# Decayed linear attention and a sine MLP on one core: new orders for all queues, other engines and load sizes in the opening, and the last tile's first store on SyncE

## The chip, the cores and the metric

One NeuronCore of a Trainium2 (trn2) chip. The metric is the device time of one execution in microseconds; the kernel before was run three times and its median is quoted. A profile is of one execution, which has its own time.

## The reference, cut to what matters

```python
# q, k, v: [4 batches, 8 heads, 768 positions, 64]; lam: [8]; block = 64
for b in range(12):                       # 12 blocks of 64 positions
    intra = einsum('bhic,bhjc->bhij', qb, kb) * Dmask     # lam**(i-j) where i >= j, else 0
    intra = einsum('bhij,bhjd->bhid', intra, vb)
    inter = einsum('bhid,bhde->bhie', qb * lam_pow, kv_state)      # lam**(pos+1)
    out[b] = intra + inter
    kv_state = lam**64 * kv_state + einsum('bhsd,bhse->bhde', kb * rev_pow, vb)
x = out.transpose(0, 2, 1, 3).reshape(3072, 512)
h = x @ w_in                              # 512 x 2048
g = h + sin(alpha * h)**2 / (alpha + 1e-9)
result = g @ w_out                        # 2048 x 512, float32 [3072, 512]
```

The inputs are float32; the kernel multiplies in bfloat16 and adds up in float32.

## The kernel before, in words

**The MLP.** The 3072 tokens go in six chunks c of 512. Step `Ac.m` (L1219) makes block m of 128 of the 2048 hidden features for chunk c: four matmuls over the 512 inputs, each 512 columns wide. Where its name ends in h0 or h1 it makes one half of the tokens for two blocks, with 256 columns. ACT takes the sine (`sin`, L1231), POOL, DVE or ACT squares it (`sq`, L1238 on ACT, L1239 on the others; the tables SQ0 and SQ1 say who), and DVE makes g out of the square and the PSUM (`g`, L1243), which frees the PSUM bank. Step `Bc.s.m` (L1296) adds four feature blocks into the output tile s of 128 tokens; after the fourth, ACT copies the tile out (L1312) and issues its store of 256 KB (L1315). The last tile of the last chunk, B5.3, is done in `last_tile` by column pieces instead: piece 0 has 256 columns, 1 and 2 have 128 each (CUTS). Each piece has 16 matmuls (L1264), a copy (L1272, on ACT for 0 and 2, on DVE for 1; tags o23.0 to o23.2) and a store of its own (L1275; tags st23.0 to st23.2; on ACT's queue for 0 and 2, on SP's for 1).

**The attention.** It makes x, transposed, chunk by chunk, in 24 quads t of 128 tokens by four head pairs. The first eight quads are `quad0`: quads 0 to 3 make chunk 0, 4 to 7 chunk 1. For quad t: the loads of q, k and v (`load_quad`, L780 for q, L786 for k and v; float32, tags such as "quad q3.0", "quad k2.1"); the scaling by powers of lam (`qs` L825, `ks` L838, the latter in two halves .0 and .1 where the engine table names two engines); the cast of v (`vs`, L852 on ACT, L855 elsewhere); transposes on PE of k and q (`Tk`, `Tq`, L866) and their copies out of PSUM (`cTt.1` for k, `cTt.0` for q, L869); the scores (`S`, L909) and their mask on DVE (`mask`, L914); the state's matmuls (`Z`, L926) with two copies (`Zi`, L945); the inter part (`I`, L956), the intra part (`O`, L971), the copy to x (`x`, L988); the running state on DVE (`Zt.1`, L999) and its bf16 copies (`Zs`, L1011). Quads 0 and 1 start from an empty state; 2 and 3 continue from theirs. S0 needs cT0.0, cT0.1 and the q parts; Z needs `ks` and `vs`; O needs the mask and `vs`. After x0 to x3 the A steps of chunk 0 can run: A0.4 and others begin on the half that x0 and x1 give, A0.2 needs all four. Later quads (8 to 23) are transposed by DMA (tags DT).

**Weights.** POOL issues software DMAs for w_in (tags w0, w0b, w1 to w3) and w_out (w4 to w7), which cast to bf16 on the way.

**What sets the order.** Every operation is recorded with what it reads and writes (`rec`). The class `Program` then walks through them with modelled times; each engine's sequence, including its DMA issues, is written out by hand in the table ORDER, one list for PE, DVE, ACT, POOL and SP (c0, c1, ... are the constants). The dependencies become semaphore waits. Four things follow from that table and the model's times: which PSUM bank each step gets (six banks for all but the scores of the opening); how many filler matmuls on zeros (L641) go in front of a PE step that would wait; the loads that GATE names wait for the named step before SP issues them, as does everything behind them on SP's queue; and a POOL step that the model starts less than 0.3 us after a DVE step marked `port="whole"` gets a wait for that DVE step. SP also holds back while more than 2300 descriptors of its are under way.

In PE's list of before the opening runs: Tk2, Tq1, Tq2, Tq3, Tq0, Tk0, S0, Tk1, Z1, Z0, S1, alpha T, I0, O0, I1, S2, Z3, Tk3, O1, Z2, S3, A0.4h0e (the first half of A0.4's h0), I2, A0.4h0, I3, O2, O3, A0.2h0, ... The first loads on SP are q2.0, k0.0, k2.1 (one pair of head pairs, 128 KB), q3.0, q1.0, q0.0, k2.0, v0.0, v2.0, k3.1 (the other 128 KB), v2.1, v0.1, q4.0, k6.1, v4.0, k4.0; k0.1 is issued by ACT.

Of the kernel before, what the change touches and what calls it, by code (L numbers as in the profile page):

```python
# [37 lines left out]
    ENG0=({'c': 'DVE', 'k': 'POOL', 'p': 1, 'q': ('POOL', 'DVE'), 'v': 'POOL', 'w': 'AD', 'z': 'DA'},
          {'c': ('ACT', 'DVE'), 'k': 'DVE', 'p': 2, 'q': 'DVE', 'v': 'ACT', 'w': 'DA', 'z': 'DD'},
          {'c': ('DVE', 'ACT'), 'k': ('DVE', 'POOL'), 'p': 2, 'q': 'DVE', 'v': 'ACT', 'w': 'DD', 'z': 'AD'},  # L40
          {'c': ('DVE', 'ACT'),
           'k': ('POOL', 'DVE'),
           'p': 2,
           'q': ('DVE', 'POOL'),
           'v': 'ACT',
           'w': 'DA',
           'z': 'AA'}),
    X0=('ACT', 'DVE', 'DVE', 'ACT'),
    ENG1=({'c': 'ACT', 'k': ('POOL', 'DVE'), 'p': 0, 'q': 'DVE', 's': 0, 'v': 'POOL', 'w': 'AA', 'z': 'DD'},
          {'c': ('DVE', 'ACT'),  # L50
# [6 lines left out]
           'z': 'AD'},  # L57
          {'c': ('DVE', 'ACT'),
           'k': ('POOL', 'DVE'),
           'p': 2,  # L60
           'q': ('POOL', 'DVE'),
           's': 0,
           'v': 'ACT',
           'w': 'DD',
           'z': 'AA'},
          {'c': ('ACT', 'DVE'),
           'k': ('DVE', 'POOL'),
           'p': 1,
           'q': ('DVE', 'POOL'),
           's': 0,  # L70
           'v': 'DVE',
           'w': 'AD',
           'z': 'DD'}),
# [1381 lines left out]
```

## Time and profile before

| | us |
|---|---|
| median of 3 runs | 213.82 (213.73 to 213.84) |
| the profiled execution | 213.67 |
| its span, first to last instruction | 211.8 |
| ACT busy (L1231, the sines, 65.7 of it) | 128.7 |
| DVE busy (L1243, the g steps, 70.2 of it) | 128.5 |
| POOL busy (L1239, the squares, 70.6 of it) | 120.7 |
| matmuls of the A steps, L1219 | 88.1 |
| matmuls of the B steps, L1296 | 83.6 |
| fillers on zeros, L641, 45 groups | 10.7 |

The granted TensorE clock of the profiled execution was 0.998. The page's second part cuts the span into 40 slices of 5.3 us and gives each engine's busy tenths in each:

```profile
PE   7798999999999999999999999999999999999994
PEld 5455756555774555444554455454544544444454
DVE  4598899678889971285753475474556521456700
ACT  3146899835599755767648756757786434646231
POOL 3772174511537772899945899687397335144500
```

The first four to five digits of each row are the opening; the last is the end. A row of the timeline has the start, the length, the engine, the line, the operation with output and inputs, the shapes, the count of merged instructions, and in brackets the idle time ahead of it and what ended that.

### The profile page before, as it was taken

How to read it: one execution, taken by the hardware profiler on the slowest of the kernel's cores; microseconds unless marked ns; L12 is line 12 of the kernel's file. 1: busy time of each engine (PE TensorE's matmuls, PEld its weight loads, DVE VectorE, ACT ScalarE, POOL GpSimd, SP SyncE). 2: the span in 40 equal slices, each digit the busy share in tenths (PEclk: the TensorE clock that was granted, in tenths of full speed). 3: DMA queues.
4: the chain of work that ended last, by engine and by line, in shares of the span. 5: the costliest groups of instructions: out<-in, count | busy, mean ns of one | idle time of the engine just before them, and what ended most of it. 6: DMA issues, size and time to landing. Idle time of an engine off the chain costs nothing.

```text
span 211.8 us, 5201 instructions
## 1 busy us (share of the span) xinstructions
PE 202.6 (96%) x2108; PEld 108.9 (51%) x2139; DVE 128.5 (61%) x229; ACT 128.7 (61%) x246; POOL 120.7 (57%) x135
## 2 busy tenths in 40 slices
PE   7798999999999999999999999999999999999994
PEld 5455756555774555444554455454544544444454
DVE  4598899678889971285753475474556521456700
ACT  3146899835599755767648756757786434646231
POOL 3772174511537772899945899687397335144500
PEclk9999999999999999999999999999999999999999
DMA  6999999998999968899779999957033011101214
GB/s 182 314 238 235 208 251 237 216 223 169 244 182 197 190 117 190 200 199 197 189 154 209 198 183 240 177 137 171 3 99 148 4 50 50 53 0 50 101 54 149
DMA packets 86491, 33.92 MB, mean 160 GB/s; under 512 B 68274, under 2 KB 83522, under 8 KB 86466
## 3 DMA queue, kind: packets, MB, share of 16 engines
q1 hardware_dynamic: 77552, 22.88, 55.3%
q0 software_dynamic: 4752, 4.19, 12.1%
q10 hardware_dynamic: 4162, 6.50, 8.7%
q8 instruction: 17, 0.28, 0.6%
q14 instruction: 8, 0.07, 0.1%
HBM read 27.27 MB, written 6.29 MB: 158 GB/s over the span
## 4 chain that ended last, share of the span: by engine, by line
PE 85%; DVE 6%; DMA 2%; issue 2%; ACTq 1%; SPq 1%; ACT 1%; POOL 0%; POOLq 0%
PE M_ps L1219 39%; PE M_ps L1296 36%; DMA q<-in_q_dram 2%; PE M_ps L1120 2%; PE M_ps L1100 1%; DVE gT L1243 1%; PE A_ps L1080 1%; PE M_ps L866 1%; PE M_ps L971 1%; DVE S_m L1092 1%; DVE S_m L914 1%; PE M_ps L956 1%; PE M_ps L1264 1%; DVE q2o L825 1%; PE A_ps L909 1%
## 5 line engine op out<-in xcount | busy, mean ns | idle before, releaser
L1239 POOL TENSOR_TENSOR u<-t 128x512 bf16<-128x512 bf16 x69 | 70.6, 1041 | 55.0 <-ACT t L1231 51.7
L1243 DVE SCALAR_TENSOR_TENSOR gT<-u,r_sb,M_ps 128x512 bf16<-128x512 bf16 (+1 forms) x108 | 70.2, 684 | 45.1 <-POOL u L1239 43.8
L1219 PE MATMUL M_ps<-xT,w 128*128 128x512 bf16 (+1 forms) x425 | 88.1, 355 | 0.6 <-DVE gT L1243 0.2
L1296 PE MATMUL M_ps<-w,gT 128*128 128x512 bf16 x347 | 83.6, 379 | 2.5 <-issue 1.9
L1231 ACT ACTIVATE t<-M_ps,alpha_sb 128x512 bf16<-128x512 f32 (+1 forms) x108 | 65.7, 640 | 27.7 <-PE M_ps L1219 26.0
L1219 PEld LDWEIGHTS M_ps<-xT,w 128*128 128x128 bf16 x432 | 41.4, 98 | 40.1 <-DVE gT L1243 0.5
L1296 PEld LDWEIGHTS M_ps<-w,gT 128*128 128x128 bf16 x368 | 34.3, 98 | 39.2 <-DVE gT L1243 0.4
L1044 POOL TENSOR_TENSOR qk<-k,Lk 128x512 bf16<-128x512 f32 x16 | 16.6, 1044 | 9.9 <-DMA k<-in_k_dram 9.9
L1092 DVE TENSOR_TENSOR S_m<-A_ps,maskl 128x768 bf16<-128x768 f32 x16 | 15.3, 955 | 8.5 <-PE A_ps L1080 8.4
L1312 ACT COPY osb<-M_ps 128x512 f32<-128x512 f32 x20 | 11.7, 585 | 13.4 <-PE M_ps L1296 13.4
L1044 POOL TENSOR_TENSOR qk<-q,Lq 128x512 bf16<-128x512 f32 x16 | 16.6, 1041 | 2.2 <-DMA q<-in_q_dram 2.2
L1172 ACT CAST xT<-M_ps 128x512 bf16<-128x512 f32 x16 | 9.4, 586 | 13.3 <-PE A_ps L1080 11.4
L641 PE MATMUL M_ps<-zeros 128*128 128x512 bf16 (+1 forms) x45 | 10.7, 390 | 1.4 <-DVE zeros L702 1.2
L1195 ACT CAST Zq<-Zf 64x256 bf16<-64x256 f32 x24 | 9.6, 400 | 1.4 <-DVE Zf L1185 0.7
L914 DVE TENSOR_TENSOR S_m<-A_ps,maskq 128x1024 bf16<-128x1024 f32 x8 | 9.7, 1212 | 1.0 <-PE A_ps L909 0.5
L1239 DVE TENSOR_TENSOR u<-t 128x512 bf16<-128x512 bf16 x13 | 7.3, 560 | 4.4 <-ACT t L1231 4.4
L1055 ACT CAST v<-v 128x512 bf16<-128x512 f32 x16 | 9.7, 618 | 0.3 <-DMA v<-in_v_dram 0.2
L838 POOL TENSOR_TENSOR qk<-k,Lk 128x256 bf16<-128x256 f32 (+1 forms) x7 | 4.9, 703 | 8.6 <-DMA k<-in_k_dram 8.0
L1238 ACT ACTIVATE u<-t 128x512 bf16<-128x512 bf16 x14 | 8.7, 636 | 0.3
L869 ACT COPY qkT<-M_ps 128x512 bf16<-128x512 bf16 x5 | 2.9, 587 | 7.3 <-PE M_ps L866 7.3
L641 PEld LDWEIGHTS M_ps<-zeros 128*128 128x128 bf16 x48 | 4.6, 122 | 4.4 <-issue 1.7
L1189 DVE TENSOR_TENSOR Zf<-M_ps,Zf 128x256 f32<-128x256 f32 x10 | 4.2, 418 | 4.2 <-ACT xT L1172 4.2
(87 smaller groups left out, 139.8 us busy)
## 6 DMA issues: line engine op xcount, KB each, us to landing
out_dram<-osb ACTq DMA_DIRECT2D x23, 256.0 KB, 2.8
q<-in_q_dram SPq DMA_DIRECT2D x20, 256.0 KB, 4.8
k<-in_k_dram SPq DMA_DIRECT2D x34, 128.0 KB, 4.2
v<-in_v_dram SPq DMA_DIRECT2D x32, 128.0 KB, 4.0
v<-in_v_dram SPq DMA_DIRECT2D x8, 256.0 KB, 8.2
w<-in_moe_w_out_dram POOLq DMA_DIRECT2D x4, 512.0 KB, 11.5
k<-in_k_dram SPq DMA_DIRECT2D x6, 256.0 KB, 10.5
...
```

The costliest lines, as they stand in the source:

```text
L641: last = e.matmul(m_ps[i][:, 0:c], zeros[:, 0:128], zeros[:, 0:c])
L914: rec("DVE", lambda e: e.tensor_tensor(S_m[jm][:, :, :].rearrange("p (h a b) c -> p h a (b c)", h=2, a=2), Av().rearrange("p h (a x) -> p ...
L1044: rec(en, lambda e, L=L, gs=slice(g0, g0 + m): e.tensor_tensor(o[:, :, gs], i[:, :, gs], L, ALU.mult), *(((0.65, 0.58) if en == "DVE" else ...
L1055: rec("ACT", lambda e: e.copy(o, i), 0.613, 0.51, reads=rd, writes=[f"v2.{c}"], tag=f"vs{t}")
L1092: rec("DVE", lambda e: e.tensor_tensor(S_m[jm][:, :, :].rearrange("p (a b) c -> p a (b c)", a=4)[:, :, 0:192], A_ps[:, :, :].rearrange("p ...
L1195: rec(en, lambda e, rows=rows, en=en: (e.copy if en == "ACT" else e.tensor_copy)(Zq[jj][rows, :, rows], Zf[jj][rows, :, :].rearrange("p i ...
L1219: last = e.matmul(m_ps[vb.i][:, N * i:N * i + N], w1[:, kc, 128 * mm:128 * (mm + 1)], xT[x][:, kc, ts], start=(kc == 0 and i == 0), stop=( ...
L1231: rec("ACT", lambda e, i=i, mm=mm: e.activation(t16[tt][:, N * i:N * i + N], m_ps[vb.i][:, N * i:N * i + N], ACTF.Sin, scale=alpha_sb[:, m ...
L1239: return e.tensor_tensor(u16[tt][:, :], t16[tt][:, :], t16[tt][:, :], ALU.mult)
L1243: rec("DVE", lambda e, i=i, mm=mm: e.scalar_tensor_tensor(out=gT[g][:, mm, ts], in0=u16[tt][:, N * i:N * i + N], scalar=r_sb[:, mm:mm + 1] ...
L1296: last = e.matmul(m_ps[vb.i], gT[g][:, m, 128 * s4:128 * (s4 + 1)], w2[:, m, :], start=(m == 0 or (split and m == 8)), stop=(m == NM - 1 o ...
L1312: rec("ACT", lambda e: e.copy(osb[o][:, :], m_ps[vb.i]), 0.585, 0.48, reads=[vb.key], writes=[f"o.{o}"], frees=[vb], tag=f"o{gsi}")
```

## The change

The tables in TUNE get other values, the constants' DVE steps get a mark, and one line of `last_tile` names another engine. No step of the computation is added or taken away.

- LOADS0: the two loads of 128 KB "quad k2.1" and "quad k3.1" become one of 256 KB with the tag "quad k2.1", in the third place of SP's list.
- ENG0, ENG1, X0: who does which step of the opening. x1 and x2 go from DVE to ACT; vs0 from POOL to ACT, qs1 from DVE to POOL; cT0.0, Zi0.0, Zi1.0, Zi1.1 and Zs0.1 from DVE to ACT; cT2.1, cT1.0, cT3.1, Zi0.1 and Zi2.0 from ACT to DVE; ks4.0 from POOL to DVE and ks4.1 from DVE to POOL; some more for quads 4 to 7.
- SQ1: sq1.7 (ACT) and sq1.14 (DVE) go to POOL.
- GATE: k4.0 waits for Tk1, q6.0 for Tk3, v4.1 for O0, v6.0 for Tk2 (before: v4.0 for O2, k6.0 for mask3, v6.1 for Tk3). The table's other keys name no step that is recorded before their load and do nothing.
- EARLY: the places in the table SEQ at which the four quads of the opening are recorded; the order on the engines is ORDER's.
- ORDER: new lists for all five queues.
- `port="whole"` on the DVE steps that make the constants (memsets, copies, one add).
- `last_tile`: the store of piece 0 is on SP's queue; in ORDER the pieces' matmuls come as 1, 0, 2 (before 0, 2, 1), and ACT's list ends with o23.0, o23.2, st23.2.

```diff
-    SQ1=('ACT', 'DVE', 'POOL', 'POOL', 'ACT', 'POOL', 'POOL', 'ACT', 'DVE', 'ACT', 'ACT', 'POOL', 'POOL', 'ACT',
-         'DVE', 'DVE'),
+    SQ1=('ACT', 'DVE', 'POOL', 'POOL', 'ACT', 'POOL', 'POOL', 'POOL', 'DVE', 'ACT', 'ACT', 'POOL', 'POOL', 'ACT',
+         'POOL', 'DVE'),
...
-    EARLY=(0, 3, 1, 2),
+    EARLY=(0, 2, 2, 2),
...
-    GATE={'k6.0': 'mask3', 'q4.1': 'mask0', 'q6.1': 'A0.2', 'v4.0': 'O2', 'v6.0': 'A0.2', 'v6.1': 'Tk3'},
+    GATE={'k4.0': 'Tk1', 'q4.1': 'Tk2', 'q6.0': 'Tk3', 'q6.1': 'A0.2', 'v4.0': 'A0.2', 'v4.1': 'O0', 'v6.0': 'Tk2'},
...
-            ('q', 0, 1, 1), ('k', 1, 2, 1), ('v', 1, 2, 2), ('k', 1, 3, 1), ('v', 1, 0, 2), ('k', 0, 2, 2),
-            ('v', 0, 2, 2)],
+            ('q', 0, 1, 1), ('v', 1, 2, 2), ('k', 1, 2, 2), ('v', 1, 0, 2), ('k', 0, 2, 2), ('v', 0, 2, 2)],
...
-    X0=('ACT', 'DVE', 'DVE', 'ACT'),
+    X0=('ACT', 'ACT', 'ACT', 'ACT'),
...
-    ORDER={'ACT': ['lam', 'c0', 'quad k0.1', 'c11', 'c13', 'c14', 'cT2.1', 'alpha in', 'c17', 'vs1', 'cT1.0', 'Zi0.1',
-                   'alpha', 'x0', 'vs3', 'c16', 'Zs0.0', 'cT3.1', 'vs2', 'Zi3.1', 'Zs1.1', 'Zi3.0', 'Zi2.0', 'c29',
-                   'sin0.4h0', 'x3', 'sin0.2h0', 'sin0.5h0', 'sin0.7', 'sin0.3h0', 'sin0.1', 'sin0.4h1', 'sq0.1',
+    ORDER={'ACT': ['lam', 'c0', 'quad k0.1', 'c11', 'c14', 'c16', 'c13', 'vs0', 'cT0.0', 'alpha in', 'vs1', 'Zi0.0',
+                   'vs3', 'Zi1.0', 'Zi1.1', 'x0', 'Zs0.0', 'x1', 'Zi3.1', 'Zi3.0', 'Zs1.1', 'vs2', 'alpha', 'Zs0.1',
+                   'c17', 'c29', 'sin0.4h0', 'sin0.5h0', 'x2', 'x3', 'sin0.2h0', 'sin0.3h0', 'sin0.7', 'sin0.1',
...
-           'DVE': ['c1', 'c9', 'c25', 'c7', 'c2', 'c20', 'c23', 'c10', 'c12', 'qs1', 'c22', 'qs3', 'ks2.0', 'qs2',
-                   'cT2.0', 'cT3.0', 'c15', 'cT0.0', 'cT0.1', 'ks1', 'c19', 'c26', 'mask0', 'cT1.1', 'Zi1.0', 'Zi0.0',
-                   'Zi1.1', 'mask1', 'ks3.1', 'c31', 'Z0.1', 'mask2', 'x1', 'Zs0.1', 'c27', 'c24', 'Zi2.1', 'Zs1.0',
-                   'mask3', 'Z1.1', 'x2', 'Z3.1', 'qs4', 'Z2.1', 'Zs2.0', 'sq0.4h0', 'g0.4h0', 'g0.5h0', 'sq0.2h0',
+           'DVE': ['c2', 'c26', 'c1', 'c7', 'c23', 'c19', 'c9', 'c10', 'c25', 'c20', 'c15', 'c12', 'c27', 'qs3',
+                   'qs2', 'ks2.0', 'ks3.1', 'cT2.0', 'cT3.0', 'cT2.1', 'c24', 'cT0.1', 'cT1.0', 'Zi0.1', 'ks1',
+                   'mask0', 'cT1.1', 'mask1', 'Z0.1', 'cT3.1', 'Zs1.0', 'mask2', 'Z1.1', 'Zi2.1', 'Zi2.0', 'mask3',
+                   'sq0.4h0', 'ks4.0', 'c31', 'g0.4h0', 'Z2.1', 'Z3.1', 'qs4', 'sq0.2h0', 'g0.5h0', 'g0.2h0',
...
-           'PE': ['ln lam', 'Tk2', 'Tq1', 'Tq2', 'Tq3', 'Tq0', 'Tk0', 'S0', 'Tk1', 'Z1', 'Z0', 'S1', 'alpha T', 'I0',
-                  'O0', 'I1', 'S2', 'Z3', 'Tk3', 'O1', 'Z2', 'S3', 'A0.4h0e', 'I2', 'A0.4h0', 'I3', 'O2', 'O3',
+           'PE': ['ln lam', 'Tq2', 'Tq3', 'Tk2', 'Tq1', 'Tk0', 'Tq0', 'Z0', 'S0', 'Z1', 'I0', 'Tk3', 'Tk1', 'O0',
+                  'S1', 'I1', 'O1', 'alpha T', 'Z3', 'S2', 'I3', 'Z2', 'S3', 'A0.4h0e', 'A0.4h0', 'I2', 'O2', 'O3',
...
+                  'B5.1.1', 'B5.0.1', 'B5.1.2', 'B5.1.3', 'B5.2.3', 'B5.0.2', 'B5.0.3', 'B5.3.1', 'B5.3.0',
+                  'B5.3.2'],
-           'POOL': ['c6', 'c3', 'c5', 'c18', 'c4', 'c8', 'c21', 'ks2.1', 'ks0', 'w1', 'qs0', 'w0b', 'w0', 'c28',
-                    'ks3.0', 'vs0', 'w3', 'c30', 'w2', 'w4', 'sq0.7', 'ks7.1', 'qs6', 'w5', 'sq0.15', 'w6', 'vs4',
-                    'w7', 'ks4.0', 'sq0.2h1', 'qs5', 'ks5.0', 'ks6.0', 'ks8', 'qs8', 'ks9', 'qs9', 'sq1.4h0',
+           'POOL': ['c6', 'c3', 'c4', 'c28', 'c18', 'c5', 'qs1', 'c8', 'ks0', 'ks2.1', 'w0b', 'w1', 'qs0', 'w0', 'w3',
+                    'ks3.0', 'w2', 'w4', 'w5', 'c21', 'c30', 'w6', 'w7', 'sq0.7', 'qs6', 'sq0.15', 'ks4.1', 'vs4',
+                    'sq0.2h1', 'qs5', 'ks7.1', 'ks5.0', 'ks6.0', 'ks9', 'ks8', 'qs9', 'qs8', 'sq1.4h0', 'sq1.0h1',
...
-                  'quad v0.0', 'quad v2.0', 'quad k3.1', 'quad v2.1', 'quad v0.1', 'quad q4.0', 'quad k6.1',
-                  'quad v4.0', 'quad k4.0', 'load v4.0e', 'quad q6.0', 'quad k6.0', 'quad v6.0', 'quad k4.1',
+                  'quad v0.0', 'quad v2.0', 'quad v2.1', 'quad v0.1', 'quad k4.0', 'quad q4.0', 'quad k6.1',
+                  'load v4.0e', 'quad v4.0', 'quad q6.0', 'quad k6.0', 'quad k4.1', 'quad v6.0', 'quad v6.1',
...
-            zd = rec("DVE", lambda e: e.memset(zeros[:, :], 0.0), 0.2, writes=["zeros"])
-            rec("DVE", lambda e: e.memset(ones[:, :], 1.0), 0.1, writes=["ones"])
+            zd = rec("DVE", lambda e: e.memset(zeros[:, :], 0.0), 0.2, writes=["zeros"], port="whole")
+            rec("DVE", lambda e: e.memset(ones[:, :], 1.0), 0.1, writes=["ones"], port="whole")
...
-                rec("SP" if y % 2 else "ACT", lambda e, a=a, b=b: e.dma_start(out[row0:row0 + 128, a:b], osl[:, a:b]),
+                rec("SP" if y < 2 else "ACT", lambda e, a=a, b=b: e.dma_start(out[row0:row0 + 128, a:b], osl[:, a:b]),
```

The kernel after has 23 lines fewer ahead of its functions, so a line of after is 23 lower than the same line of before.

More of the change, by code (lines that the diff above doesn't have):

```diff
@@ L27 @@
     HALF1=3,
-    EARLY=(0, 3, 1, 2),
+    EARLY=(0, 2, 2, 2),
     NARROW=4,
     CUTS=(0, 256, 384, 512),
-    GATE={'k6.0': 'mask3', 'q4.1': 'mask0', 'q6.1': 'A0.2', 'v4.0': 'O2', 'v6.0': 'A0.2', 'v6.1': 'Tk3'},
+    GATE={'k4.0': 'Tk1', 'q4.1': 'Tk2', 'q6.0': 'Tk3', 'q6.1': 'A0.2', 'v4.0': 'A0.2', 'v4.1': 'O0', 'v6.0': 'Tk2'},
     SPLIT=(1, 1, 0, 1),
     LOADS0=[('k', 1, 0, 2, 'ACT'), ('q', 0, 2, 1), ('q', 0, 3, 1), ('k', 0, 0, 2), ('q', 0, 0, 1), ('v', 0, 0, 2),
-            ('q', 0, 1, 1), ('k', 1, 2, 1), ('v', 1, 2, 2), ('k', 1, 3, 1), ('v', 1, 0, 2), ('k', 0, 2, 2),
-            ('v', 0, 2, 2)],
+            ('q', 0, 1, 1), ('v', 1, 2, 2), ('k', 1, 2, 2), ('v', 1, 0, 2), ('k', 0, 2, 2), ('v', 0, 2, 2)],
     LOADSQ1=[('v', 1, 0, 2), ('v', 0, 0, 2), ('q', 0, 2, 2), ('v', 0, 2, 2), ('k', 0, 0, 2), ('k', 1, 0, 2),
              ('v', 1, 2, 2), ('k', 0, 2, 2), ('q', 0, 0, 2), ('k', 1, 2, 2)],
[L38 to L47, printed above, removed]
-    X0=('ACT', 'DVE', 'DVE', 'ACT'),
-    ENG1=({'c': 'ACT', 'k': ('POOL', 'DVE'), 'p': 0, 'q': 'DVE', 's': 0, 'v': 'POOL', 'w': 'AA', 'z': 'DD'},
-          {'c': ('DVE', 'ACT'),
+    ENG0=({'c': ('ACT', 'DVE'), 'k': 'POOL', 'p': 1, 'q': ('POOL', 'DVE'), 'v': 'ACT', 'w': 'AA', 'z': 'AD'},
[3 rows of a table added]
+    X0=('ACT', 'ACT', 'ACT', 'ACT'),
+    ENG1=({'c': ('ACT', 'DVE'), 'k': ('DVE', 'POOL'), 'p': 0, 'q': 'DVE', 's': 0, 'v': 'POOL', 'w': 'AA', 'z': 'AA'},
+          {'c': ('ACT', 'DVE'),
            'k': ('POOL', 'DVE'),
@@ L56 @@
            'w': 'AA',
[L57 to L73, printed above, removed]
+           'z': 'DA'},
+          {'c': 'DVE', 'k': ('POOL', 'DVE'), 'p': 1, 'q': ('POOL', 'DVE'), 's': 0, 'v': 'ACT', 'w': 'AA', 'z': 'AA'},
+          {'c': 'ACT', 'k': ('DVE', 'POOL'), 'p': 2, 'q': ('DVE', 'POOL'), 's': 0, 'v': 'DVE', 'w': 'AD', 'z': 'DD'}),
     X1=('BOTH', 'BOTH', 'BOTH', 'ACT'),
@@ L711, in consts @@
                 writes=["E_i3"])
-            rec("DVE", lambda e: e.memset(maskf[:, :], 0.0), 0.2, writes=["maskf"])
+            rec("DVE", lambda e: e.memset(maskf[:, :], 0.0), 0.2, writes=["maskf"], port="whole")
             rec("POOL", lambda e: e.affine_select(
@@ L716, in consts @@
             P.fill_after = (zd,)
-            rec("DVE", lambda e: e.tensor_copy(E_f[:, :], E_i[:, :]), 0.15, reads=["E_i", "E_i2", "E_i3", "E_i4"], writes=["E_f"])
+            rec("DVE", lambda e: e.tensor_copy(E_f[:, :], E_i[:, :]), 0.15, reads=["E_i", "E_i2", "E_i3", "E_i4"], writes=["E_f"], port="whole")
             rec("DVE", lambda e: e.tensor_scalar_add(E_f[64:128, 8:8 + 2 * NB], E_f[64:128, 8:8 + 2 * NB], -64.0), 0.15, reads=["E_f"],
-                writes=["E_f4"])
+                writes=["E_f4"], port="whole")
             rec("ACT", lambda e: e.activation(lnlam[:, :], lam_1[:, :], ACTF.Ln), 0.2,
@@ L739, in consts @@
             rec("DVE", lambda e: e.tensor_copy(maskq[64:128, :, :], maskq[0:64, :, :]), 0.15, reads=["maskq.0"],
-                writes=["maskq.1"])
-            rec("DVE", lambda e: e.memset(maskl[:, :], 1.0), 0.15, writes=["maskl"])
+                writes=["maskq.1"], port="whole")
+            rec("DVE", lambda e: e.memset(maskl[:, :], 1.0), 0.15, writes=["maskl"], port="whole")
             rec("POOL", lambda e: e.affine_select(
@@ L747, in consts @@
             rec("DVE", lambda e: e.tensor_copy(maskl[64:128, :], maskl[0:64, :]), 0.15, reads=["maskl"],
-                writes=["maskl"])
+                writes=["maskl"], port="whole")
             for i in range(2):
-                rec("DVE", lambda e, i=i: e.memset(Zq[i][:, :, :], 0.0), 0.27, writes=[f"Zq.{i}.{z}.{h}" for z in range(2) for h in range(2)])
+                rec("DVE", lambda e, i=i: e.memset(Zq[i][:, :, :], 0.0), 0.27, writes=[f"Zq.{i}.{z}.{h}" for z in range(2) for h in range(2)], port="whole")
             for i in range(RZ):
-                rec("DVE", lambda e, i=i: e.memset(Zi[i][:, :, :], 0.0), 0.2, writes=[f"Zi.{i}.0", f"Zi.{i}.1"])
+                rec("DVE", lambda e, i=i: e.memset(Zi[i][:, :, :], 0.0), 0.2, writes=[f"Zi.{i}.0", f"Zi.{i}.1"], port="whole")
             rec("POOL", lambda e: e.affine_select(
```

169 rows, old and new, of tables (ENG0, ORDER) are left out of this document.

## The prediction

> **What bounds the kernel now.** I read the page first, then PE's waits and the busy time by windows, then the timeline of each engine in the first 25 us, then the last 7 us, and last the DMA queues.
>
> ```profile
> span 211.8 us, 5201 instructions
> ...
> PE 202.6 (96%) x2108; PEld 108.9 (51%) x2139; DVE 128.5 (61%) x229; ACT 128.7 (61%) x246; POOL 120.7 (57%) x135
> ```
> ```profile
> PE M_ps L1296 <- issue: 1.9, 12, 0.2
> ```
> ```profile
> 22.70:50.00 27.30, 26.98 (x239) 15.47 (x237) 23.35 (x49) 20.92 (x42) 10.55 (x13) 1.00 1.15 220
> ...
> sum 184.30, PE 181.11 PEld 95.06 DVE 112.13 ACT 118.30 POOL 109.78; mean PE 25.87 PEld 13.58 DVE 16.02 ACT 16.90 POOL 15.68
> ```
> In the page PE is busy 202.6 of 211.8 us. The windows (stretch, then busy us of PE, PEld, DVE, ACT and POOL, clock, DMA share, GB/s) add up 22.7 to 207 us: PE works 181.1 of 184.3 us. The longest entry of its waits in that stretch is the second fence: 12 pauses, none over 0.2 us. That stretch holds the large matmuls, which the change only reorders. So there are three parts: an opening in which PE waits for loads, scales, masks and copies, and runs filler matmuls on zeros meanwhile; 184 us in which nothing can be won but a stall can be added; and an end behind the last matmul. The profiled execution took 213.67 us, 1.87 more than its span and 0.15 less than the median of the runs, 213.82.
>
> **The opening, part by part.** The rows of PE, DVE, ACT and POOL (start, length, work; in brackets the idle time before and what ended it):
>
> ```profile
> 11.63 0.42 PE L909 MATMUL A_ps<-qTo,qkT 64*64 64x128 bf16 x16
> 11.98 0.82 PE L641 MATMUL M_ps<-zeros 128*128 128x512 bf16 x3
> ...
> 13.20 0.60 PE L641 MATMUL M_ps<-zeros 128*128 128x512 bf16 x2
> 13.73 0.31 PE L926 MATMUL M_ps<-v,qk 64*64 64x64 bf16 x8
> 13.98 0.39 PE L641 MATMUL M_ps<-zeros 128*128 128x512 bf16 x1
> ...
> 16.46 1.04 PE L641 MATMUL M_ps<-zeros 128*128 128x512 bf16 x4
> 17.43 0.31 PE L926 MATMUL M_ps<-v,qk 64*64 64x64 bf16 x8
> 17.67 0.40 PE L866 MATMUL M_ps<-ident,qk 128*128 128x128 bf16 x4
> 18.00 0.42 PE L971 MATMUL M_ps<-S_m,v 64*64 64x128 bf16 x16
> ...
> 19.32 0.25 PE L909 MATMUL A_ps<-qTo,qkT 64*64 64x128 bf16 x2
> ...
> 19.73 0.83 PE L1219 MATMUL M_ps<-xT,w 128*128 128x256 bf16 x6
> 20.93 0.27 PE L956 MATMUL M_ps<-qTo,Zq 128*128 128x128 bf16 x2 [0.37 <-ACT Zi L945]
> ...
> 21.48 0.28 PE L956 MATMUL M_ps<-qTo,Zq 128*128 128x128 bf16 x2
> ...
> 21.91 0.42 PE L971 MATMUL M_ps<-S_m,v 64*64 64x128 bf16 x16
> ...
> 22.73 1.27 PE L1219 MATMUL M_ps<-xT,w 128*128 128x256 bf16 x10
> ```
> ```profile
> 7.08 1.12 DVE L825 TENSOR_TENSOR q2o<-q,Lq 128x512 bf16<-128x512 f32 x1 [1.75 <-DMA q<-in_q_dram]
> ...
> 13.68 0.41 DVE L869 COPY qkT<-M_ps 128x512 bf16<-128x512 bf16 x1
> ...
> 14.83 1.23 DVE L914 TENSOR_TENSOR S_m<-A_ps,maskq 128x1024 bf16<-128x1024 f32 x1
> ...
> 18.58 0.69 DVE L988 CAST xT<-M_ps 128x512 bf16<-128x512 f32 x1 [0.76 <-PE M_ps L926]
> ...
> 20.40 0.28 DVE L1011 CAST Zq<-M_ps 64x128 bf16<-64x128 f32 x1
> ...
> 23.73 0.69 DVE L825 TENSOR_TENSOR q2o<-q,Lq 128x512 bf16<-128x512 f32 x1
> ```
> ```profile
> 11.29 0.62 ACT L852 CAST v<-v 128x512 bf16<-128x512 f32 x1 [0.35 <-DMA v<-in_v_dram]
> 11.82 0.58 ACT L869 COPY qTo<-M_ps 128x512 bf16<-128x512 bf16 x1
> ...
> 15.61 0.59 ACT L988 CAST xT<-M_ps 128x512 bf16<-128x512 f32 x1 [0.52 <-PE M_ps L926]
> ```
> ```profile
> 6.03 1.62 POOL L838 TENSOR_TENSOR qk<-k,Lk 128x256 bf16<-128x256 f32 x2 [2.96 <-DMA k<-in_k_dram]
> ...
> 9.29 1.04 POOL L825 TENSOR_TENSOR q2o<-q,Lq 128x512 bf16<-128x512 f32 x1 [0.72 <-DVE q2o L825]
> ```
> The long run of A matmuls (L1219 x10, its first is A0.2) starts at 22.73; from there PE hardly stops. I walk the new order to that point with these rows.
>
> *Loads.* DVE waited for q3's load until 7.08, ACT for v2's until 11.29. From q3 to v2 SP's queue holds five more loads of 256 KB (q1, q0, k2, v0, v2): 0.84 us each. Now k2.1, the third load, brings two pairs instead of one, 128 KB more (the k3.1 behind v2 goes). So q3 to v2 come 0.42 later: q3 at 7.5, q0 at 9.2, v0 at 10.45 + 0.42 = 10.9.
>
> *To the first scores, S0.* vs0, the cast of v0, moves from POOL to ACT, ahead of cT0.0, which S0 needs: 10.9 to 11.5, then cT0.0 (0.58) to 12.1. qs0 on POOL (9.2 + 1.04) and Tq0 behind it are done by 10.8 and hidden. On PE Z0 now stands before S0: Z0 at 11.55 takes 0.25 (13.73 to 13.98), two fillers 0.53 (13.20 to 13.73), S0 starts at **12.33**, 0.70 later than at present (11.63).
>
> *To mask1.* S0 0.35, four fillers 0.97 (16.46 to 17.43), Z1 0.25, I0 0.2 and Tk3 0.23 (estimates: 17.67 to 18.00 is 0.33 with a change of tiling); Tk1 starts at 14.33 and ends 0.40 on. cT1.1 on DVE 0.41, S1 0.42, mask1 15.7 to **16.9**, where it ends at 16.06 at present. So far the change loses 0.85.
>
> *The gain.* At present four fillers, Z3 and Tk3 stand between mask1 and O1, which starts at 18.00. In the new order Tk3 is long done, Z3 follows O1, and the five fillers ahead of O1 (1.1 us) end about when mask1 does. O1 starts at 16.97, 1.03 earlier. The copy x1 can start 0.58 behind it (18.00 to 18.58), and moves from DVE to ACT, 0.59 for 0.69: 17.55 to 18.14. Then Zs1.0 on DVE 0.28, mask2 18.45 to 19.65, and S3 at 19.7 (at present 19.32). Behind S3 come both halves of A0.4 end to end, 8 matmuls at 0.107 (an estimate from the run at 22.73: 1.27 less a tail of 0.2, by ten); at present I2 stands between them, with 0.37 of waiting for Zi. From S3 0.41 (19.32 to 19.73), A 0.86, I2 0.43 (21.48 to 21.91), O2 and O3 0.82 (21.91 to 22.73): the long run starts at **22.2** instead of 22.73. mask3, three small copies of 0.28 behind mask2, ends at 21.6, 0.1 before O3 wants it: it hides only just.
>
> By the walk the opening gains 0.53. Pauses of 0.2 to 0.4 between small steps, like that 0.37, don't show in a walk; I expect one of half its size and take **0.35**. Bounds: a gain of 0.9 if the larger k2.1 costs its followers nothing, a loss of 0.2 if two such pauses come.
>
> *DVE against POOL.* qs3 took 1.12 at 7.08, beside POOL's L838 pair (6.03 to 7.65); the same form took 0.69 at 23.73. POOL now runs qs1 (1.04) ahead of that pair, and by its rows is done near 7.5, as q3 lands. If it is late, qs3 pays its 0.43 again, in a branch with 0.7 us of slack, since cT0.0 waits for vs0 anyhow: I cost it at nothing. The Trainium skill, SBUF — State Buffer, section "Who interferes with whom", has a VectorE instruction with two SBUF inputs contend with a GpSimd one that reads SBUF, and the one that issues second blocks until the other ends. By that rule qs3 could wait out a whole POOL step of 1.04, the slack would be overdrawn by 0.3, and the sum would be 213.6 at the median; the trace has 0.43 on top, less than a whole step, so I leave this inside rival 1.
>
> *What else moves.* sq1.7 and sq1.14 go to POOL, slower there, but POOL is 57% busy and PE has six PSUM banks to go on with: nothing, and up to 0.4 if a bank comes late. The port marks on the constants add waits of POOL on DVE before 3 us, when all wait for loads: nothing. Two narrow fillers go ahead of the logarithm's matmul, which waits for ACT: nothing.
>
> **The end.**
>
> ```profile
> 205.32 3.70 PE L1264 MATMUL M_ps<-w,gT 128*128 128x256 bf16 x48
> ...
> 207.67 1.57 ACTq L1275 DMA_DIRECT2D out_dram<-osl  x1
> 209.06 0.29 DVE L1272 COPY osl<-M_ps 128x128 f32<-128x128 f32 x1 [8.05 <-PE M_ps L1264]
> 209.28 0.27 ACT L1272 COPY osl<-M_ps 128x128 f32<-128x128 f32 x1 [1.64 <-PE M_ps L1264]
> ...
> 209.58 0.34 ACTq L1275 DMA_DIRECT2D out_dram<-osl  x1
> ```
> PE ends at 209.02. ACT copies a piece whose matmuls were long done only at 209.28, because its queue hung 1.57 us in issuing the first piece's store; the copied piece's own store goes at 209.58, 0.56 behind PE. In the new kernel SP issues that first store, and ACT copies the piece that PE finishes last, 0.04 behind PE (209.02 to 209.06), and stores it 0.30 after that copy's start, 0.34 behind PE. Gain **0.22**, if ACT's queue is free. Its last two large stores stand some 2.5 us before PE's end, 0.4 apart; should they hang by 1.57, they end 0.5 before that last store. Bounds: a gain of 0.25, and a loss of 1 if the last issue itself hangs.
>
> **Sum.** 0.35 + 0.22 = 0.57 off 213.67 gives 213.1; the median stands 0.15 higher, 213.25: I say **213.3**.
>
> **The rivals.**
>
> 1. *Only the end gains.* Pauses eat what O1 wins and the long run starts at 22.6 to 22.8: 213.5 to 213.8. For it: S3 is 0.35 later than at present, and the whole gain lies behind it. Against: from S3 on PE waits for nothing but mask3.
>
> 2. *Slower: q4's load comes late.* SP now holds k4.0 until Tk1 has run (about 14.7) and brings it ahead of q4. DVE reaches qs4 (at 23.73 at present) in order, and behind it stand the gT steps that free PE's banks.
>
> ```profile
> q0 software_dynamic: 1758, 1.23, 79.7%
> q1 hardware_dynamic: 1584, 1.05, 43.7%
> ```
> ```profile
> q1 hardware_dynamic: 1098, 0.50, 34.4%
> ```
> These are the queues' packets, MB and share at 12.5 to 22.5 (q1 is SP's, q0 POOL's, with the weights), then q1's at 24 to 30 us. In the first stretch SP moved 1.05 MB in 10 us, as much as v0.1, k4.0 and q4 of the new order make together: q4 near 22.5. At the second rate, 83 KB/us, it takes 12.3 us, 24.8, and 25.7 if SP idles 0.9 at the gate: 1.9 late, of which I give PE three quarters, as DVE is 86% busy there (23.35 of 27.30): 1.4, so 214.7. It eats the gain from 24.6 on. POOL also issues the last weights early, so that q6 (qs7, then Tq7 near 41 us) runs the same risk. The Trainium skill, DMA: Bandwidth & Descriptors, section "Queues, rings and completion order", says that each DMA engine goes round-robin between rings, a packet at a time. By that rule SP keeps its turn however much POOL has queued, and q4 lands by the first rate, with no loss; the trace has both rates, so the rule alone doesn't decide.
>
> 3. *ACT's issue hangs at the end too.* Then the last store gains nothing, or loses: 213.5 to 213.9.
>
> **How the numbers follow.** The forecast (both gains, 212.7 to 213.4) has 0.5; rivals 1 and 3 together 0.28; rival 2, or another stall in the long stretch, 0.22. The range, 212.6 to 214.3, takes in the opening's upper bound, rivals 1 and 3 and the milder half of 2. A measurement tells 0.2% (0.43 us) from no change: faster by more 0.5, within it 0.28, slower 0.22.
>
> **What would show it.** Line numbers of the new kernel are 23 lower. Right: vs0 on ACT starts near 10.9, S0 near 12.3, O1 near 17.0, the long run of A matmuls near 22.2, and ACT's last copy within 0.1 of PE's last matmul. Wrong: O1 after 17.6 or S3 after 20.2; DVE idle before q2o near 24 with a DMA as releaser; PE pauses over 0.3 between 23 and 45 us; an ACT store issue over 1 us at the end.

## The result, and the profile after

The changed kernel is slower: 217.36 us (median of four executions) beside 213.77 for the kernel before in the same series; ratio **1.0139**, 95% interval 1.0109 to 1.017, from the three of them that took 216.10, 217.10 and 217.62 us. A second series of the same kernel gave 217.73 (217.38 to 218.03), ratio 1.0189 (1.0171 to 1.0207). The fourth took 538.07 us, with matmuls of 512 columns 0.62 us apart from beginning to end (0.216 in the second series) at a clock of 1.0 in its records; it is left out of the ratio, and the profile shown here is that of the second series, an execution of 218.01 us.

The page of the kernel after, its first lines, then the waits of PE and of DVE (us in total, times, longest):

```profile
span 216.2 us, 5225 instructions
...
PE 207.1 (96%) x2137; PEld 108.6 (50%) x2137; DVE 125.5 (58%) x221; ACT 128.7 (60%) x252; POOL 123.6 (57%) x137
```
```profile
PE M_ps L1196 <- DVE gT L1220: 2.3, 1, 2.3
```
```profile
DVE q2o L802 <- DMA q<-in_q_dram: 6.0, 2, 3.2
```

PE's share is 96% as before, which says nothing: the page counts a matmul as busy at whatever pace it runs. The waits say more. Before, the long stretch of PE had no pause over 0.2 us; now one A step (L1196) waited 2.3 us for a g step on DVE, and DVE waited 3.2 us for a load of q. The windows put both in one place (length, then busy us of PE, PEld, DVE, ACT and POOL, clock, DMA share, GB/s):

```profile
22.50:30.00 7.50, 5.18 (x29) 2.50 (x27) 4.27 (x12) 4.68 (x10) 1.39 (x2) 0.92 1.19 229
30.00:40.00 10.00, 10.00 (x58) 5.48 (x56) 8.80 (x18) 8.54 (x17) 2.88 (x4) 0.89 1.20 220
```

Each of the four compute engines stands still for a part of the 7.5 us from 22.5 to 30 (PE for 2.3), and the granted clock, 1.00 elsewhere, falls in these two windows. The chain of waits of the same kernel tells it in order (start, length, what):

```profile
13.82 0.46 PE M_ps L843 x8
...
14.30 0.37 SPq L763
...
14.71 12.76 DMA q<-in_q_dram
...
27.49 0.69 DVE q2o L802
28.18 0.34 DVE u L1216
28.52 0.40 DVE gT L1220
...
28.97 8.68 PE M_ps L1196 x40
```

Tk1 (L843) ends, and SP, which held k4.0 for it (the gate), issues k4.0 at 14.30 and q4.0 at 14.71. q4.0 lands 12.76 us later, at 27.47; qs4 runs on DVE at once; behind it a square and a g step free a PSUM bank, and PE, stopped since 26.65, goes on at 28.97. This is rival 2 of the prediction, at a higher price than it was given.

PE by single microseconds (length, busy us and count, clock, DMA share, GB/s):

```profile
26.00:27.00 1.00, 0.65 (x3) 1.00 1.20 218
27.00:28.00 1.00, 0.00 (x0) 1.00 1.21 218
28.00:29.00 1.00, 0.03 (x1) 0.90 1.18 214
29.00:30.00 1.00, 1.00 (x3) 0.50 1.22 208
30.00:31.00 1.00, 1.00 (x4) 0.50 1.21 195
31.00:32.00 1.00, 1.00 (x4) 0.50 1.23 198
32.00:33.00 1.00, 1.00 (x6) 0.90 1.22 196
```

Behind the pause PE is busy in full, but a microsecond holds three or four matmuls in place of six to eight: by the trace they start about 0.427 us apart in place of 0.216, and from the first, at 28.97, to the ninth, at 32.28, that costs 1.6 us. The clock's record has the fall from 28.79 to 32.20. So the loss has two parts, the pause of 2.3 and the half pace of 1.6 after it.

The opening itself came out better than forecast, and the end as forecast. PE of the kernel after, then DVE, ACT and SP at the places that the prediction named:

```profile
11.98 0.42 PE L886 MATMUL A_ps<-qTo,qkT 64*64 64x128 bf16 x16
...
16.54 0.42 PE L948 MATMUL M_ps<-S_m,v 64*64 64x128 bf16 x16
...
18.68 0.27 PE L933 MATMUL M_ps<-qTo,Zq 128*128 128x128 bf16 x2 [0.44 <-ACT Zq L988]
...
19.49 0.25 PE L886 MATMUL A_ps<-qTo,qkT 64*64 64x128 bf16 x2
...
22.04 2.23 PE L1196 MATMUL M_ps<-xT,w 128*128 128x256 bf16 x15
```
```profile
7.26 1.45 DVE L802 TENSOR_TENSOR q2o<-q,Lq 128x512 bf16<-128x512 f32 x2 [2.81 <-DMA q<-in_q_dram]
...
15.26 1.23 DVE L891 TENSOR_TENSOR S_m<-A_ps,maskq 128x1024 bf16<-128x1024 f32 x1 [0.53 <-PE A_ps L886]
```
```profile
10.53 0.62 ACT L829 CAST v<-v 128x512 bf16<-128x512 f32 x1 [5.57 <-DMA v<-in_v_dram]
```
```profile
210.08 3.70 PE L1241 MATMUL M_ps<-w,gT 128*128 128x128 bf16 x48
213.81 0.27 ACT L1249 COPY osl<-M_ps 128x128 f32<-128x128 f32 x1 [0.52 <-PE M_ps L1241]
214.11 0.34 ACTq L1252 DMA_DIRECT2D out_dram<-osl  x1
211.49 2.19 SPq L1252 DMA_DIRECT2D out_dram<-osl  x2
```

The long run of A matmuls starts at 22.04 (22.73 before), and ACT's last copy 0.03 behind PE's last matmul (0.26 before). The 0.69 won by 22.04 stands against 3.9 lost between 26.65 and 32.3.

### The profile page after: what moved, and what is told of

Read it like the earlier page. It is cut to its first block, busy times and chain, and to the rows that moved or that the text cites. A ratio compares the mean times of both kernels' runs of the same rounds, so it can differ in the third digit from the quotient of the medians.

```text
span 536.3 us, 5193 instructions
## 1 busy us (share of the span) xinstructions
PE 521.3 (97%) x2105; PEld 195.6 (36%) x2137; DVE 126.7 (24%) x221; ACT 132.6 (25%) x252; POOL 123.4 (23%) x137
## 4 chain that ended last, share of the span: by engine, by line
PE 97%; issue 2%; DVE 0%; ACT 0%
PE M_ps L1196 42%; PE M_ps L1273 40%; PE M_ps L618 4%; PE M_ps L1241 2%; PE M_ps L843 2%; PE M_ps L1077 1%; PE M_ps L1097 1%; PE A_ps L1057 1%; PE M_ps L933 1%; PE A_ps L886 1%; PE M_ps L948 1%; PE M_ps L903 1%; PE M_ps L1108 1%; DVE S_m L891 0%; PE A_ps L699 0%
## 5 line engine op out<-in xcount | busy, mean ns | idle before, releaser
L1196 PE MATMUL M_ps<-xT,w 128*128 128x512 bf16 (+1 forms) x421 | 230.6, 763 | 3.9 <-issue 3.9
L1273 PE MATMUL M_ps<-w,gT 128*128 128x512 bf16 x350 | 219.2, 835 | 6.0 <-issue 5.7
L1216 POOL TENSOR_TENSOR u<-t 128x512 bf16<-128x512 bf16 x71 | 73.1, 1040 | 306.3 <-ACT t L1208 305.6
L1196 PEld LDWEIGHTS M_ps<-xT,w 128*128 128x128 bf16 x432 | 72.8, 170 | 148.1 <-issue 132.9
L1273 PEld LDWEIGHTS M_ps<-w,gT 128*128 128x128 bf16 x368 | 61.1, 170 | 136.4 <-issue 134.5
L1021 POOL TENSOR_TENSOR qk<-k,Lk 128x512 bf16<-128x512 f32 x16 | 16.6, 1043 | 42.9 <-issue 29.6
L618 PE MATMUL M_ps<-zeros 128*128 128x512 bf16 (+1 forms) x43 | 20.0, 658 | 2.5 <-DVE zeros L679 1.4
L1021 POOL TENSOR_TENSOR qk<-q,Lq 128x512 bf16<-128x512 f32 x16 | 16.6, 1041 | 0.0
L891 DVE TENSOR_TENSOR S_m<-A_ps,maskq 128x1024 bf16<-128x1024 f32 x8 | 9.8, 1223 | 16.9 <-PE A_ps L886 16.8
L1077 PEld LDWEIGHTS M_ps<-qkT,Zq 128*128 128x128 bf16 x56 | 8.8, 175 | 12.0 <-issue 11.5
L1077 PE MATMUL M_ps<-qkT,Zq 128*128 128x128 bf16 x56 | 11.5, 386 | 0.0
L1057 PE MATMUL A_ps<-qkT 64*64 64x128 bf16 (+1 forms) x256 | 10.8, 325 | 0.0
L1241 PE MATMUL M_ps<-w,gT 128*128 128x128 bf16 (+1 forms) x48 | 9.8, 434 | 0.0
```

The source lines that it names most:

```text
L618: last = e.matmul(m_ps[i][:, 0:c], zeros[:, 0:128], zeros[:, 0:c])
L1021: rec(en, lambda e, L=L, gs=slice(g0, g0 + m): e.tensor_tensor(o[:, :, gs], i[:, :, gs], L, ALU.mult), *(((0.65, 0.58) if en == "DVE" else ...
L1057: last = e.matmul(Av[ps, h, a, ek, 0:64 if ek else 128], T[rows, 1, a, ek, ps], T[rows, 0, a, i, 64 * ek:128])
L1077: last = e.matmul(bank(i)[:, a, :], Zq[jj][:, 2 * i + a, :], T[:, 0, a, i, :], start=(a == 0), stop=False, skip_group_check=True)
L1196: last = e.matmul(m_ps[vb.i][:, N * i:N * i + N], w1[:, kc, 128 * mm:128 * (mm + 1)], xT[x][:, kc, ts], start=(kc == 0 and i == 0), stop=( ...
L1216: return e.tensor_tensor(u16[tt][:, :], t16[tt][:, :], t16[tt][:, :], ALU.mult)
```

## The experiments

Theory: the change to the opening and to the end gains; the loss comes from q4.0's load alone, which the gate on k4.0 holds back, and from the clock that falls behind the pause. Rivals: POOL's weights, issued earlier, take the bandwidth; the end gains nothing; the port marks or the clock by itself cost time.

**The kernel after again.** No edit.

> The kernel after, unchanged, for more times and a profile. Its first times were 216.1, 217.1 and 217.6 us, and 538 once, with every matmul of 512 columns at 0.60 us. Theory A (a late load, rival 2): the times stay near 217, and the profile shows DVE or PE waiting 1 us or more for q4, q6 or a weight between 23 and 45 us, at a granted clock of 0.998 as before. Theory B (clock): the profile shows no such wait; a stretch of the opening has matmuls at twice their length for about 3 us, the granted clock is 0.992, and times of runs with 0.992 lie 1 us or more above those with a higher clock.

Measured: 217.73; the profile above. Each theory is half right: the wait for q4 that theory A names is there (3.2 us on DVE), but at 0.992; the 3.4 us at half the clock that theory B names are there, but behind a wait, which B had ruled out. The granted clock of the whole execution was 0.992 in this profile and in the executions of 217.1 and 217.6 us, and 1.0 in that of 216.1: the halving does not come each time. The other three of the second series have 0.992 too.

**The end alone.** In the kernel before (the last two lines give the ends of the lists in ORDER):

```diff
-                rec("SP" if y % 2 else "ACT", lambda e, a=a, b=b: e.dma_start(out[row0:row0 + 128, a:b], osl[:, a:b]),
+                rec("SP" if y < 2 else "ACT", lambda e, a=a, b=b: e.dma_start(out[row0:row0 + 128, a:b], osl[:, a:b]),
...
-  PE  'B5.3.0', 'B5.3.2', 'B5.3.1'    ACT 'o23.0', 'st21', 'st23.0', 'o23.2', 'st23.2'   SP 'st23.1'
+  PE  'B5.3.1', 'B5.3.0', 'B5.3.2'    ACT 'st21', 'o23.0', 'o23.2', 'st23.2'             SP 'st23.1', 'st23.0'
```

> The kernel before with the change of the end alone: the first piece's store on SP, the pieces in the order 1, 0, 2, and ACT's last copy and store last. The forecast's term for the end: 0.22 us faster (213.55), ACT's last copy within 0.1 us of PE's last matmul, no issue over 1 us on ACT at the end. Rival 3: ACT's last issue hangs all the same, 213.5 to 214.2, with an issue of 1 us or more just ahead of the end.

Measured: 213.67 beside 213.76, ratio 0.9991 (0.9973 to 1.0009). The median alone can't tell 0.2 from nothing. In the profile the span ended 2.40 us behind PE's last matmul (2.78 in the kernel before), ACT's last copy stood 0.03 behind PE, and the issues that hung (2.19 us for two) were SP's and over before PE's last matmul.

**qs4 later on DVE.** In the kernel after:

```diff
-  'Z2.1', 'Z3.1', 'qs4', 'sq0.2h0', 'g0.5h0', 'g0.2h0', 'g0.3h0', 'g0.7', 'g0.1', 'Zs3.1', 'c22',
+  'Z2.1', 'Z3.1', 'sq0.2h0', 'g0.5h0', 'g0.2h0', 'g0.3h0', 'g0.7', 'g0.1', 'Zs3.1', 'qs4', 'c22',
```

> The kernel after with one step moved on DVE: qs4, which waits for q4's load, goes from ahead of the squares and g steps of A0.2 and A0.5 to behind them (behind Zs3.1). Loads are as in after, where q4 landed at 27.47 us. Theory L (the load of q4 is late, and qs4 waits for it at the head of DVE's queue while the g steps that free PSUM banks stand behind it): PE's pause of 2.32 us at 26.65 goes, the granted clock stays at 1.0 or 0.998, and the time is 213.76 less the 0.69 by which the long run of A matmuls came earlier and less 0 to 0.3 for the end: 212.8 to 213.1. Rival C (the clock falls or a bank is late whatever qs4 does): 215.5 or more, with a pause of over 1 us between 24 and 33 us.

Measured: 215.41 (214.95 to 215.62), ratio 1.0075 (1.0053 to 1.0098). The pause of 2.32 and the half pace are gone (clock 1.0), and 2.3 us with them, so qs4 at the head of DVE's queue was what stopped PE. But the expected 213 did not come: the theory named one step behind one load, and there were more. POOL's waits and PE's of this run, then DVE's rows:

```profile
POOL q2o L802 <- DMA q<-in_q_dram: 3.6, 2, 2.4
```
```profile
PE M_ps L843 <- DVE q2o L802: 1.4, 2, 1.0
PE M_ps L1196 <- DVE gT L1220: 0.8, 1, 0.8
PE M_ps L1273 <- DVE gT L1220: 0.7, 3, 0.3
```
```profile
27.83 0.83 DVE L988 CAST Zq<-Zf 64x128 bf16<-64x128 f32 x1
28.67 0.69 DVE L802 TENSOR_TENSOR q2o<-q,Lq 128x512 bf16<-128x512 f32 x1
...
30.06 2.85 DVE L1220 SCALAR_TENSOR_TENSOR gT<-u,r_sb,M_ps 128x512 bf16<-128x512 bf16 x5
```

PE's pause of 0.8 at 30.13 ended with g0.0, the first step of the last row. Two things made it late. Zs3.1 (L988) took 0.83 us beside POOL's qs6, which needs the same load of q4.0 and ran from 27.53; without the gate, with qs6 done by then, Zs3.1 takes 0.22. And qs4 itself (0.69) stood ahead of g0.0 now, where the edit had put it. Later q6.0, behind q4.0 on SP's queue, landed at 42.15 (38.46 without the gate); qs7 on DVE waited 0.9 and Tq7 on PE 0.3 for it near 43. The gate had delayed the whole queue, not one load.

**The gate taken away.** In the kernel after, once the order is fixed, so that nothing else moves:

```diff
         order = self.schedule()
+        by = {o.tag: o for o in order}
+        by['quad k4.0'].deps.discard(by['Tk1'])
```

> The kernel after with one wait taken from SP's queue: k4.0 no longer waits for Tk1; order and all else as in after. Theory G (the gate holds k4.0 and q4 back until 14.3 us, and a queue that then holds one load moves at half the rate): k4.0 is issued near 8 and q4 near 9 us, q4 lands by 23 us, PE's pause at 26.65 goes, 212.8 to 213.3. Rival W (POOL's weights, which are issued earlier than before, take the bandwidth): q4 still lands after 25 us, PE still pauses by 0.5 us or more, 214.5 or more.

Measured: **213.05** (212.58 to 213.36) beside 213.70, ratio 0.9963 (0.9948 to 0.9977): faster than both kernels. By the trace k4.0 was issued at 8.84 and landed at 19.84, q4.0 at 9.72 and 23.57. DVE runs qs4 without waiting, and PE's longest wait behind 22 us is 0.2:

```profile
24.34 0.68 DVE L804 TENSOR_TENSOR q2o<-q,Lq 128x512 bf16<-128x512 f32 x1
```

q4.0 landed half a microsecond later than forecast for theory G (by 23), and rival W is out: POOL's weights were issued as early as in after, and PE did not pause. From 213.05 to the 217.73 of after it is 4.7: the pause 2.3, the half pace 1.6, and 0.8 more, in which falls one wait of 0.9 for a transposing DMA (L1077, at 131 us) that only the profile of after has.

Why the gate costs so much more than the time that it holds is in the queues' packets (packets, MB, share; q1 is SP's, q0 POOL's). The kernel after from 16 to 18 us and from 18 to 20:

```profile
q0 software_dynamic: 649, 0.38, 134.4%
...
q1 hardware_dynamic: 3, 0.00, 0.4%
```
```profile
q0 software_dynamic: 293, 0.29, 85.5%
q1 hardware_dynamic: 273, 0.14, 34.1%
```

and the kernel without the gate from 16 to 18:

```profile
q0 software_dynamic: 354, 0.23, 76.5%
q1 hardware_dynamic: 358, 0.18, 45.1%
```

With the gate, SP's queue runs dry at 15.35 us and moves nothing until 17.96: a load issued at 14.30 shows its first packets 3.7 us later. As soon as both queues hold loads they move about as many packets each: 293 to 273, 354 to 358. So SP cannot catch up. The Trainium skill, DMA: Bandwidth & Descriptors, section "Queues, rings and completion order", has each DMA engine go round-robin between rings a packet at a time; the equal counts agree with it, though counts don't show how many in a row each queue sends. Packets, not bytes, are what a load costs here: without the gate q4.0 (512 KB) landed 3.7 us behind k4.0, and k6.1, with half the bytes in the same 512 packets, 3.7 behind q4.0.

**POOL's weights later.** In the kernel after, with its gate, w5, w6 and w7 moved behind sq0.7 and qs6:

```diff
+        for w, o in (('w4', 'w2'), ('w5', 'sq0.7'), ('w6', 'qs6'), ('w7', 'w6')):
+            order.remove(by[w])
+            order.insert(order.index(by[o]) + 1, by[w])
```

> The kernel after with the gate left as it is, but with POOL's issues of w5, w6 and w7 back behind its first squares, where they stand in before: w5 behind sq0.7, w6 behind qs6. Theory G: nothing changes for q4, since w3, w2 and w4 fill POOL's queue until 30 us either way: q4 at 27 to 28 us, 216 to 218 us, or 0.5 above it as w5 and w6 come later. Rival W: q4 lands 2 us or more earlier and the time falls below 215.

Measured: 216.91 (216.49 to 217.46), ratio 1.0149 (1.012 to 1.0178). q4.0 landed at 28.52, 12.84 us behind its issue (12.76 in after), DVE waited 3.29 us for it, PE paused 2.4. No help; rival W falls here too, for w5 to w7 (the earlier weights stand as in after). The profile is not like that of after in all else: from the third load on SP's loads came a microsecond or more later, and its queue ran dry only from 18.2 to 19.0. In all four executions the clock stayed at 1.0 although the pause was as long as in after.

**q4 late in the kernel before.** One entry in GATE:

```diff
-    GATE={'k6.0': 'mask3', 'q4.1': 'mask0', ...
+    GATE={'q4.0': 'O2', 'k6.0': 'mask3', 'q4.1': 'mask0', ...
```

> The kernel before with one wait added: q4's load waits for O2, so that SP issues it at 22.2 us in place of 9.0. Nothing else is moved. Theory L: q4 lands near 27, qs4 holds DVE from 23.7 on, PE pauses for 2 to 2.5 us near 27 us and its clock is halved for about 3.4 us behind the pause, which costs 1.7 more: 213.76 + 2.2 + 1.7 = 217.7, or 216 in executions in which the clock holds. Rival: six PSUM banks carry PE over the wait, and the time stays below 215.

Measured: 218.84 (218.25 to 220.61), ratio 1.0252 (1.0211 to 1.0293); expected 217.7. q4.0 was issued at 22.70 and landed at 28.23, later than forecast (near 27). DVE's wait, PE's wait, and PE's windows of this run:

```profile
DVE q2o L825 <- DMA q<-in_q_dram: 5.8, 2, 4.2
```
```profile
PE M_ps L1219 <- DVE Zf L999: 2.6, 1, 2.6
```
```profile
30.00:31.00 1.00, 1.00 (x4) 0.50 1.13 236
31.00:32.00 1.00, 1.00 (x4) 0.50 1.14 289
```

The late load (and with it k6.1, which stands behind it on SP's queue), put into the kernel that had no such trouble, gives the same picture: a wait on DVE, a pause on PE, then half pace. The six PSUM banks carry PE for about 1.6 of DVE's 4.2 us. Pause and half pace make 2.6 + 1.7 = 4.3 of the 5.1; the other 0.8 wasn't traced to a step.

**Fillers in the pause.** In the kernel after, ahead of A0.0, ten matmuls on zeros into the scores' PSUM, which is free there:

```diff
+        f = Op('PE', lambda e: self.fill(e, 10, -1, 512), 0, 0, -1)
+        f.deps = {by['mask3']} | set(self.fill_after)
...
+        order.insert(order.index(by['A0.0']), f)
```

> The kernel after with ten matmuls of 512 columns on zeros put on PE ahead of A0.0, the step at which it paused by 2.32 us; they write the PSUM of the scores, which is free there. The load of q4 stays late. Theory K (part of the loss is the clock: in the profile of after the eight matmuls behind the pause ran 0.427 us apart in place of 0.216, because PE had idled): PE has no idle time there, no matmul behind it runs at half pace, and 1.6 us of the loss go: 217.7 becomes 216.1, the granted clock 1.0 in every execution. Rival: the halving has nothing to do with the idle time: it stays, at 217 or more.

Measured: 215.72 (215.41 to 215.98 in ten executions), ratio 1.0074 (1.0047 to 1.0101). PE of this run at the place where it had paused:

```profile
27.00:28.00 1.00, 1.00 (x6) 1.00 1.20 217
28.00:29.00 1.00, 0.90 (x5) 1.00 1.18 214
29.00:30.00 1.00, 0.97 (x5) 1.00 1.23 212
```

The load is as late as in after (27.53) and no useful work is added, yet 2.0 us are won against the 217.73 of the second series. PE takes up its useful work at 29.03 as in after (28.97), only at full pace, and the granted clock is 1.0 in all ten executions. So the half pace followed from PE's idling, and its price is 1.6 us by the profile of after and 2.0 by these medians.

**The gate opened 3 us earlier.** In the kernel after:

```diff
+        by['quad k4.0'].deps.discard(by['Tk1'])
+        by['quad k4.0'].deps.add(by['Z0'])
```

> The kernel after with k4.0's wait moved from Tk1 (14.2 us) to Z0 (about 11.4 us). Theory G in its full form: what the gate costs is the time in which SP's queue is empty, here from 15.2 to 17.7 us, since a load's first packets moved 3.6 us behind its issue; a gate that opens 3 us earlier is followed by packets near 15.2, just as the queue runs dry, and costs nothing: q4 lands at 23.5 to 24.5 us and the time is that without the gate, 213.0 to 213.3. Rival: any wait there pushes the whole queue back by its own length: q4 lands near 25.5, 214 to 215.

Measured: 213.14 beside 213.75, ratio 0.9964 (0.9934 to 0.9994). k4.0 was issued at 11.56 and landed at 19.99, q4.0 at 23.86: 0.3 later than with no gate, for an issue 2.3 to 2.7 later. In this profile the queue is empty only from 15.37 to 15.60. Theory G holds in its full form in this pair: the gate that left the queue empty for 0.2 us cost nothing that shows, the one that left it empty for 2.6 cost 4.7 us.

**No gate, and the end of before.** The kernel without the gate, with `"SP" if y % 2 else "ACT"` and the pieces in the order 0, 2, 1.

> The kernel after without k4.0's wait (213.05 us) and with the end of before: the first piece's store on ACT, the pieces in the order 0, 2, 1. By the forecast the end is worth 0.22 us: 213.3, the span's end 2.8 us behind PE's last matmul in place of 2.4. Rival 3 (the end gains nothing): 213.05 and 2.4.

Measured: 213.37 beside 213.75, ratio 0.9978 (0.9956 to 1.0001); 0.32 above the kernel with the new end, with intervals that overlap. The span ended 3.0 us behind PE's last matmul (2.8 with the new end). With the pair of the second experiment (2.78 and 2.40) the end is worth 0.2 to 0.4 in profiles and 0.1 to 0.3 in medians, none of it clear of noise by itself; the forecast of 0.22 lies among them.

**No gate, no port marks.** The kernel without the gate and without `port="whole"` on the constants.

> The kernel after without k4.0's wait and without the port marks on the constants, so that POOL's steps and issues before 12 us no longer wait for those DVE steps; one filler of 512 columns fewer ahead of Z1. By the forecast the marks cost nothing: 213.05, within 0.3. Rival: the marks hold POOL's qs1 and ks0 back, and the opening comes 0.3 to 0.6 us earlier without them.

Measured: 213.13, ratio 0.9975 (0.9948 to 1.0003), 0.08 from the kernel with the marks. They cost nothing that shows, as forecast.

## Why the prediction was wrong

**The step that failed** is in rival 2, and it decided the sign: "q4 near 22.5. At the second rate, 83 KB/us, it takes 12.3 us, 24.8, and 25.7 if SP idles 0.9 at the gate", at a chance of 0.22 and a price that gave 214.7. It came at 27.47. The idling at the gate was mis-sized, 0.9 for 2.6 us, and the price left out the clock.

1. *The idling at the gate.* The estimate let SP go on from 12.5 us, with 0.9 of idling at most. The queue was empty for 2.6 us, because k4.0's first packets came 3.7 us behind its issue. The gate's own time was read, and not this delay. The trace of before has it: v4.0, held by its gate, was issued at 22.48, with SP's queue empty, and from 24 to 26 us only POOL's queue moved; SP's first packets came at 26.04, 3.6 us behind the issue.

```profile
22.48 0.37 SPq L786 DMA_DIRECT2D v<-in_v_dram  x1
```
```profile
q0 software_dynamic: 401, 0.40, 120.9%
```

2. *The rate.* Its sum held, by luck. Less the 2.6 us of emptiness, the three loads took 12.4 us from 12.5 to 27.47; the second rate gave 12.3 (12.6 with the fence's own 1.05 MB and 0.50 MB in 6 us). But the stretch from 24 to 30 us, from which that rate was read, has those 2 us with an empty queue in it. The shares within the sum were wrong, as they were taken in bytes where packets count: k4.0 has half the bytes of q4.0 and as many packets, so that "k4.0 ahead of q4.0" put almost a whole load's time in front. The sentence on the Trainium skill's rule (DMA: Bandwidth & Descriptors, "Queues, rings and completion order") said that SP keeps its turn and q4 then lands by the first rate, with no loss. The rule held and the conclusion did not: the turn was kept, but there was nothing to send for 2.6 us, and without the gate, with the turn kept all along, q4 landed at 23.57 and not at 22.5.
3. *The price of a pause.* Three quarters of DVE's wait was right: 2.32 of 3.20. What was left out is the clock: eight matmuls at half pace, 1.6 us. The kernel before pauses 0.76 us at most between its first fillers and the end, so its trace could not show it.

With a landing at 27.47, 3.7 behind the 23.73 that it reckoned from, the prediction's own working would have given 213.25 + 0.75 × 3.7 = 216.1 without the clock and 217.7 with it; measured 217.4 to 217.7. The chain of events was named; its likelihood was not worked out. The moment at which SP's queue runs dry (v0.1's landing, at 16.57 in the trace of before) lies behind the gate's opening, forecast for 14.7, and by itself shows no idling; with 3.6 us from issue to packets the queue comes out empty for 1.7 us, from 16.6 to 18.3, and rival 2 at 215.3, outside the range.

**The opening**: right in mechanism and, over all profiles, in size. "q3 to v2 come 0.42 later" by the larger k2.1: v0's cast started at 10.53 (forecast 10.9), v0.0 having landed at 10.50 by the trace, only 0.10 later than in before. That is the scatter of two profiles: with the loads of before v0.0 landed at 10.13, 10.20 and 10.40 in the three profiles there are, with those of after at 10.50 to 10.90 in seven and 11.48 in one (the execution of 538 us aside), and the medians are 0.4 apart. The early landing runs through the walk: S0 at 11.98 (12.33), mask1's end at 16.49 (16.9), O1 at 16.54 (16.97). From there two pauses of the kind that was allowed for appear (0.44 for Zs on ACT, 0.25 for alpha), so S3 is 0.2 early instead of 0.4: 19.49 (19.7), and the long run starts at 22.04 (22.2 by the walk). Gain 0.69; taken 0.35, walked 0.53.

**DVE against POOL**: qs3 took 0.85 us, the first 0.30 of it beside the end of POOL's ks2.1, and qs2, beside no POOL step, 0.68. So 0.16 or so was paid, in the branch that had slack; the cost of nothing was right. **Port marks**: right, shown. **sq1.7 and sq1.14 on POOL**: not tried alone; without the gate nothing is left of them in PE's waits. **The end**: right in place, and in size as far as the noise tells.

**Rivals 1 and 3** did not happen: the opening's gain reached the long run, and in the profile of after no issue on ACT's queue hung ahead of the last store.

The forecast of 213.3 lies within 0.3 of what the change gives without its gate: 213.05.
